# The rotary sum of queries and keys, moved from VectorE to an accumulating transfer on GpSimd's queue

## The chip, the cores and the metric

The kernel runs on one core of a Trainium2 chip. The metric is the time of one execution on the device in microseconds, the median of several runs. A profiled execution gives the span, which runs from the first to the last instruction, and the trace that is read below.

## What is computed

Attention over 8 batches, 8 heads, 576 positions and 64 dimensions, with a rotary embedding on queries and keys, followed by a soft mixture of 8 experts with 4 slots each:

```python
def rotate(x):
    x1, x2 = (x[..., :half], x[..., half:])
    return np.concatenate([x1 * cos - x2 * sin, x1 * sin + x2 * cos], axis=-1)
q_rot, k_rot = (rotate(q), rotate(k))
scores = scale * np.matmul(q_rot, k_rot.transpose(0, 1, 3, 2))
attn = softmax(scores); out = np.matmul(attn, v)     # cut
# then, with x = out as 4608 x 512:
logits = x @ phi                                     # 512 x 32
slot_input = softmax(logits, axis=0).T @ x
slot_out[e] = np.maximum(slot_input[e] @ w1[e], 0) @ w2[e]
result = softmax(logits, axis=1) @ slot_out
```

The rotary part is what the change touches: each of q and k is a sum of two products, the vector by cosines and its two halves swapped by signed sines.

## The kernel before

The 64 heads are taken as 32 pairs; the two heads of a pair lie in the two halves of the 128 partitions. The attention stage is a software pipeline written out by hand. A table WHEN gives every task of a pair a moment, counted in quarter pairs relative to the moment when the first block of exponentials of that pair is due; four quarter pairs are one beat, the time in which the pipeline moves on by one pair. In every beat the tasks are issued in the order of their moment modulo 4, each for the pair that is due there. Each engine runs its own instructions strictly in that order, and the transfers that one engine issues stand in that order between its other instructions.

For one pair the tasks around the change are these, in the order of their moments:

- load0 and load1 (-15.9, -14.496): SyncE (SP) issues one transfer each, 576 KB, for the queries and for the keys. A tile x_in holds both, and for each of them the vector and its swapped copy, side by side. There are two x_in tiles, so a load waits until the pair two before has been read by low.
- spin0 and spin1 (-13.466, -12.4): GpSimd multiplies x_in in place by the table of cosines and sines, in four pieces for the queries and four for the keys (L140).
- join (-9.9): VectorE adds the two products, for queries and keys at once (L144).
- high0 and high1 (-9.4817, -9.0595): ScalarE casts the sums to float16, hl (L149).
- low (-8.0): VectorE subtracts the cast from the sum, which gives the low half as float16 (L153). This is the last use of the pair's x_in.
- the tasks m.. and t0 to t8: TensorE computes scores from hl. For the m tasks VectorE takes their maxima (L175); for the t tasks ScalarE takes exponentials (L221). The tasks share three PSUM tiles.

```python
def spin(p, t, eng, cols):
    x = loaded[p][:, t]
    for c in cols:
        eng.tensor_tensor(out=x[:, :, c], in0=x[:, :, c], in1=cs_sb[:, :, c], op=ALU.mult)

def join(p, t=slice(0, 2), c=full):
    x = loaded[p]
    nc.vector.tensor_tensor(out=x[:, t, 0, c], in0=x[:, t, 0, c], in1=x[:, t, 1, c], op=ALU.add)

def high(p, t, c=full):
    ...
    nc.scalar.copy(out=halves[p][:, 1 + t, c], in_=loaded[p][:, t, 0, c])
```

Behind the attention of a pair, its softmax is normalized. ScalarE copies the sums of the exponentials out (L270), SP sends them into a tile rc (task send, L276), VectorE adds and inverts them (task recip, 7.294, L282 and L283), SP writes the reciprocals to DRAM (spread, 7.31, L289) and reads them back spread over the partitions into rb (widen, 7.3768, two transfers, L296), and GpSimd multiplies the pair's output by rb (norm, 8.706, L299).

Two moments matter for what follows. Modulo 4 norm stands at 0.706, and high0 at 2.518; load0 stands at 0.1, so SP issues it right behind widen, which stands at 3.377 of the beat before.

The start is outside the table. Pair 0 and pair 1 are loaded, multiplied, added and cast by lines of their own, with the additions on VectorE. The spins of pair 2 are issued there too. Then all tasks of the pairs 2 and 3 and so on whose moment lies before zero are issued in the order of the table, moment by moment:

```python
for when, name in sorted((when, name) for name, when in WHEN.items()):
    for p in range(NPAIR):
        if when + 4 * p < 0:
            do(name, p)
```

After the attention stage come the experts: weights from DRAM, two layers, and the output in pieces. This stage is not changed.

Of the kernel before, what the change touches and what calls it, by code (L numbers as in the profile page):

```python
# [11 lines left out]
ALU = mybir.AluOpType  # L12
# [32 lines left out]
RC = 12  # L45
PIECE = 4
WHEN = {
    "load0": -15.9, "load1": -14.496, "spin0": -13.466, "spin1": -12.4, "join": -9.9, "high0": -9.4817, "high1":
    -9.0595, "low": -8.0, "m01": -6.5262, "m10": -5.894, "m00": -5.0601, "m11": -4.7, "load_v": -3.85, "m20": -3.771,
    "m21": -3.317, "m30": -2.9, "m31": -2.7, "m_rem": -2.6642, "m_min": -2.49, "m_turn": -1.744, "m_half": -1.667,  # L50
# [13 lines left out]
def attn_softmoe(ctx, tc, qk, v, phi, w1, w2, cs, ident, sel, seg, out):  # L64
    nc = tc.nc
# [56 lines left out]
    loaded = {}  # L122
# [23 lines left out]
    def high(p, t, c=full):  # L146
        if p not in halves:
            halves[p] = stk.tile([P, 4, S], F16, name="hl")
        nc.scalar.copy(out=halves[p][:, 1 + t, c], in_=loaded[p][:, t, 0, c])  # L149
# [390 lines left out]
    def fast(task):  # L540
# [4 lines left out]
        "load1": lambda p: fetch(p, 1),  # L545
        "spin0": lambda p: spin(p, 0, nc.gpsimd, parts),
        "spin1": lambda p: spin(p, 1, nc.gpsimd, parts),
        "join": join,
        "high0": lambda p: high(p, 0),
        "high1": lambda p: high(p, 1),  # L550
        "low": low,
# [116 lines left out]
    p = NPAIR - 1  # L668
# [265 lines left out]
```

## Time and profile before

| | |
|---|---|
| time, median of 3 runs | 616.39 us (612.28 to 619.03) |
| the profiled execution | 613.56 us, of which 611.8 us are the span |
| mean granted TensorE clock | 0.959 |
| busy, share of the span | TensorE 87%, VectorE 81%, ScalarE 53%, GpSimd 52% |
| transferred | 111.63 MB, 182 GB/s over the span |

In the rows of the profile PE is TensorE, PEld its weight loads, DVE VectorE, ACT ScalarE, POOL GpSimd, SP SyncE; a name with a q behind it is that engine's sequencer, which issues transfers. A row of the timeline gives the start, the duration in us, the engine, the line of the kernel, the operation, what it writes and reads, how many instructions are merged, and in brackets how long the engine was idle before it and what ended that wait. In a row of windows stand the window, its length, the busy time of PE, PEld, DVE, ACT and POOL, the granted clock, the busy share of the DMA engines and GB/s.

### The profile page before, as it was taken

Reading aid. Unit: us, or ns where it says so; the run is one execution under the profiler, and the core shown is the slowest. Engines: PE = TensorE matmul, PEld = TensorE weight load, DVE = VectorE, ACT = ScalarE, POOL = GpSimd, SP = SyncE. Lnnn points to the kernel's source line nnn. Section 1 sums busy time; section 2 is a strip of 40 time slices with the busy share of each in tenths; the row PEclk is TensorE's granted clock in tenths of the full one; section 3 lists DMA queues with packets and bytes.
Section 4 is the critical chain, followed back from the end, with each engine's and each line's share of the span. In section 5 each row is a group of like instructions: output and inputs, shape, how many; then the busy total and the mean of one; then the engine's idle time right before and its main releaser. Section 6 shows DMA issues by size and latency. Waiting matters only on the chain.

```text
span 611.8 us, 23277 instructions
## 1 busy us (share of the span) xinstructions
PE 532.9 (87%) x10064; PEld 352.1 (58%) x10064; DVE 497.0 (81%) x729; ACT 326.9 (53%) x647; POOL 315.1 (52%) x308
## 2 busy tenths in 40 slices
PE   3668999998999899989999899898898999799981
PEld 2346666656765566666656565666566666443551
DVE  6879899999998999999998999999899874322341
ACT  2145656665665565656656566565465655324441
POOL 2668498655676566647763857658654000100000
PEclk9679999999999999999999999999899999859996
DMA  7153555555555555555555555455542246649999
GB/s 260 60 195 119 175 174 173 174 174 173 174 173 174 174 174 174 173 175 174 174 173 175 173 174 174 174 174 174 171 141 62 64 130 206 206 142 350 349 376 298
DMA packets 71734, 111.63 MB, mean 182 GB/s; under 512 B 20176, under 2 KB 47568, under 8 KB 71632
## 3 DMA queue, kind: packets, MB, share of 16 engines
q1 hardware_dynamic: 71618, 110.15, 54.5%
q8 instruction: 79, 1.29, 0.9%
q14 instruction: 23, 0.19, 0.1%
q10 hardware_dynamic: 14, 0.00, 0.0%
HBM read 99.93 MB, written 9.58 MB: 179 GB/s over the span
## 4 chain that ended last, share of the span: by engine, by line
PE 35%; DVE 26%; DMA 20%; ACT 6%; SPq 5%; issue 5%; POOL 1%; DVEq 0%; ACTq 0%
PE s_ps L220 8%; PE o_ps L236 8%; DVE nm L175 7%; DMA rc<-s 7%; DMA w_exp<-in_w 6%; DVE c_t L253 6%; DVE hl L153 5%; SPq L276 4%; ACT a_t L221 3%; PE s_ps L265 3%; DMA x_in<-in_qk 3%; PE s_ps L773 3%; DMA v_in<-in_v 2%; DVE c_t L255 2%; PE s_ps L173 2%
## 5 line engine op out<-in xcount | busy, mean ns | idle before, releaser
L140 POOL TENSOR_TENSOR x_in<-x_in,cs_sb 128x288 f32<-128x288 f32 x248 | 264.9, 1101 | 63.0 <-DMA x_in<-in_qk 38.1
L221 ACT ACTIVATE a_t<-s_ps 128x576 f32<-128x576 f32 x256 | 158.9, 649 | 97.8 <-PE s_ps L220 95.9
L175 DVE TENSOR_REDUCE nm<-s_ps 128x2 f32<-128x576 f32 x256 | 187.1, 743 | 15.1 <-PE s_ps L173 14.9
L236 PE MATMUL o_ps<-a_t,v_in 64*64 64x288 f32 x2048 | 172.4, 413 | 1.0 <-ACT xt L244 0.3
L220 PE MATMUL s_ps<-hl 64*64 64x288 f16 x3456 | 155.5, 286 | 16.4 <-DVE nm L175 15.9
L220 PEld LDWEIGHTS <-hl 64*64 64x64 f16 x3456 | 104.4, 107 | 59.9 <-issue 43.8
L299 POOL TENSOR_TENSOR xt<-xt,rb 128x576 f32<-128x576 f32 x30 | 42.8, 1425 | 141.0 <-DMA rb<-r_row 104.1
L173 PE MATMUL s_ps<-hl 64*64 64x288 f16 x1024 | 82.1, 298 | 26.0 <-DVE nm L175 20.5
L220 PE MATMUL s_ps<-peak,lift 64*64 64x288 f16 x1152 | 89.1, 284 | 0.0
L236 PEld LDWEIGHTS o_ps<-a_t,v_in 64*64 64x64 f32 x2048 | 72.9, 133 | 21.0 <-issue 7.3
L173 PEld LDWEIGHTS <-hl 64*64 64x64 f16 x1024 | 45.0, 107 | 49.1 <-issue 37.7
L149 ACT CAST hl<-x_in 128x576 f16<-128x576 f32 (+1 forms) x66 | 40.1, 650 | 33.1 <-DVE x_in L144 30.3
L270 ACT ACTIVATE s<-s_ps,bits 128x576 f32<-128x576 f32 x32 | 23.7, 740 | 58.0 <-PE s_ps L265 26.3
L144 DVE TENSOR_TENSOR x_in<-x_in 128x1152 f32<-128x1152 f32 (+2 forms) x36 | 53.4, 1483 | 0.5 <-POOL x_in L140 0.4
L253 DVE TENSOR_TENSOR c_t<-c_t,a_t 128x1152 f32<-128x1152 f32 x32 | 51.6, 1611 | 0.0
L153 DVE TENSOR_TENSOR hl<-x_in,hl 128x1152 f16<-128x1152 f32 x32 | 49.5, 1546 | 1.8 <-ACT hl L149 1.8
L253 DVE TENSOR_TENSOR c_t<-a_t 128x1152 f32<-128x1152 f32 x32 | 50.6, 1582 | 0.0
L220 PEld LDWEIGHTS <-lift 64*64 64x64 f16 x1152 | 38.1, 108 | 0.6
L265 PE MATMUL s_ps<-c_t,pick 128*32 128x288 f32 x256 | 37.1, 411 | 0.0
L265 PE MATMUL s_ps<-a_rem,pick 128*32 128x288 f32 x128 | 36.9, 411 | 0.0
L265 PE MATMUL s_ps<-a_t,pick 128*32 128x288 f32 x128 | 36.9, 411 | 0.0
L221 ACT ACTIVATE a_rem<-s_ps 128x576 f32<-128x576 f32 x32 | 20.8, 651 | 17.0 <-PE s_ps L220 17.0
(183 smaller groups left out, 597.6 us busy)
## 6 DMA issues: line engine op xcount, KB each, us to landing
x_in<-in_qk SPq DMA_DIRECT2D x62, 576.0 KB
w_exp<-in_w SPq DMA_DIRECT2D x63, 512.0 KB
v_in<-in_v SPq DMA_DIRECT2D x32, 576.0 KB
rb<-r_row SPq DMA_DIRECT2D x60, 144.0 KB
out<-w_exp SPq DMA_DIRECT2D x16, 512.0 KB
rc<-s SPq DMA_DIRECT2D x120, 4.5 KB
x_in<-in_qk SPq DMA_DIRECT2D x4, 288.0 KB
out<-w_exp SPq DMA_DIRECT2D x4, 256.0 KB
```

The lines of the kernel that those rows point to most:

```text
L140: eng.tensor_tensor(out=x[:, :, c], in0=x[:, :, c], in1=cs_sb[:, :, c], op=ALU.mult)
L144: nc.vector.tensor_tensor(out=x[:, t, 0, c], in0=x[:, t, 0, c], in1=x[:, t, 1, c], op=ALU.add)
L149: nc.scalar.copy(out=halves[p][:, 1 + t, c], in_=loaded[p][:, t, 0, c])
L153: nc.vector.tensor_tensor(out=hl[:, 0:4:3], in0=x[:, :, 0], in1=hl[:, 1:3], op=ALU.subtract)
L173: nc.tensor.matmul(s[rows[c], h, 0:HC], lhsT=hl[rows[h], QH, at:at + D], rhs=hl[rows[h], KH, half[n]], start=True, stop=True)
L175: nc.vector.tensor_reduce(out=nms[p][:, n, j:8:4], in_=s[:, :, 0:HC], axis=AX.X, op=ALU.max, negate=True)
L220: nc.tensor.matmul(s[rows[h ^ n], n, 0:HC], lhsT=lhs, rhs=rhs, start=(i == 0), stop=(i == 3))
L221: nc.scalar.activation(out=weights_of(p, b).rearrange("p (n x) -> p n x", n=2), in_=s[:, :, 0:HC], func=AF.Exp, scale=SCALE)
L236: nc.tensor.matmul(o[rows[h], n, 0:HC], lhsT=vt[r, b, n], rhs=a[r, half[n]], start=(b == 0), stop=(b == KB - 1))
L253: nc.vector.tensor_tensor(out=c, in0=c if j > 1 else ats[p, 0], in1=a, op=ALU.add)
L265: nc.tensor.matmul(s[32 * i:32 * i + 32, n, 0:HC], lhsT=pick[:, n:n + NS], rhs=m[:, half[n]], start=True, stop=True, tile_position=(0, 32 ...
L299: eng.tensor_tensor(out=xts[p], in0=xts[p], in1=rbs.pop(p), op=ALU.mult)
```

## The change

The sum of the two products is no longer an instruction on VectorE. It is a transfer that GpSimd issues: its source is the second product in x_in, its destination the first product in the same tile, and it adds to what stands there. The task's moment goes from -9.9 to -11.2, 1.3 quarter pairs forward. The first two pairs, whose lines stand outside the table, keep their addition on VectorE, so 30 of the 32 pairs are changed.

```diff
 WHEN = {
-    ... "join": -9.9, ...
+    ... "join": -11.2, ...
...
-        "join": join,
+        "join": lambda p: nc.gpsimd.dma_start(out=loaded[p][:, :, 0], in_=loaded[p][:, :, 1], accum_op=ALU.add),
```

The order of TensorE's and SP's instructions stays as it was, and so does that of ScalarE's; what its casts wait for is now the transfer. GpSimd's order changes at two kinds of place. At the start, behind the constants, it read before (L140 are the products, L299 is norm):

```order
L140 TENSOR_TENSOR x_in<-x_in,cs_sb 128x2x144 x40
L299 TENSOR_TENSOR xt<-xt,rb 128x576
L140 TENSOR_TENSOR x_in<-x_in,cs_sb 128x2x144 x8
L299 TENSOR_TENSOR xt<-xt,rb 128x576
L140 TENSOR_TENSOR x_in<-x_in,cs_sb 128x2x144 x8
```

and now reads, with the transfers as L548:

```order
L140 TENSOR_TENSOR x_in<-x_in,cs_sb 128x2x144 x24
L548 DMA x_in<-x_in 128x2x576 x2
L140 TENSOR_TENSOR x_in<-x_in,cs_sb 128x2x144 x8
L548 DMA x_in<-x_in 128x2x576
L140 TENSOR_TENSOR x_in<-x_in,cs_sb 128x2x144 x8
L299 TENSOR_TENSOR xt<-xt,rb 128x576
L548 DMA x_in<-x_in 128x2x576
```

The first 24 products are those of pairs 1, 2 and 3, eight each; the two transfers behind them are those of pairs 2 and 3, so pair 2's stands behind the products of pair 3. From the last two rows on, every beat has the same three rows in this order: the eight products of a pair, the norm of an earlier pair, and then the transfer of the pair whose products stand ahead of norm.

On VectorE the additions are gone. Its piece from the first subtractions (L153) to the first maxima of a new pair, before and now:

```order
L153 TENSOR_TENSOR hl<-x_in,hl 128x2x576
L144 TENSOR_TENSOR x_in<-x_in 128x2x576
L153 TENSOR_TENSOR hl<-x_in,hl 128x2x576
L175 TENSOR_REDUCE nm_276<-s_ps 128x2 x4
L183 TENSOR_REDUCE nm_276<-s_ps 128x2
```

```order
L153 TENSOR_TENSOR hl<-x_in,hl 128x2x576 x2
L175 TENSOR_REDUCE nm_276<-s_ps 128x2 x4
L183 TENSOR_REDUCE nm_276<-s_ps 128x2
L175 TENSOR_REDUCE nm_444<-s_ps 128x2
L187 TENSOR_REDUCE nm<-nm_276 128x9
```

The addition of pair 2 stood between the subtractions of pairs 1 and 2; now the two follow each other, and the second waits for pair 2's casts alone.

More of the change, by code (lines that the diff above doesn't have):

```diff
@@ L47 @@
 WHEN = {
-    "load0": -15.9, "load1": -14.496, "spin0": -13.466, "spin1": -12.4, "join": -9.9, "high0": -9.4817, "high1":
+    "load0": -15.9, "load1": -14.496, "spin0": -13.466, "spin1": -12.4, "join": -11.2, "high0": -9.4817, "high1":
     -9.0595, "low": -8.0, "m01": -6.5262, "m10": -5.894, "m00": -5.0601, "m11": -4.7, "load_v": -3.85, "m20": -3.771,
```

## Prediction

> **What bounds the kernel now.** I read the page first, then one row of windows over the even middle of the attention stage, then the groups by form.
>
> ```profile
> span 611.8 us, 23277 instructions
> PE 532.9 (87%) x10064; PEld 352.1 (58%) x10064; DVE 497.0 (81%) x729; ACT 326.9 (53%) x647; POOL 315.1 (52%) x308
> ...
> 100.00:400.00 300.00, 275.18 (x5725) 187.35 (x5723) 285.04 (x406) 181.98 (x362) 195.29 (x183) 1.00 0.51 170
> ...
> L144 DVE TENSOR_TENSOR x_in<-x_in 128x1152 f32<-128x1152 f32 x30 | 49.4, 1648 | 0.4 <-POOL x_in L140 0.4
> L299 POOL TENSOR_TENSOR xt<-xt,rb 128x576 f32<-128x576 f32 x30 | 42.8, 1425 | 141.0 <-DMA rb<-r_row 104.1 <-ACT a_t L221 17.6 <-DVE nm L175 13.0
> ```
>
> Over the whole span TensorE is the busier engine, but from 100 to 400 us it is VectorE: 285.04 of 300 us (95%) against 275.18 (92%) on TensorE, 61% on ScalarE and 65% on GpSimd. The DMA engines are busy half the time. The 30 rotary additions that the change takes from VectorE cost 49.4 us there, 1.65 us each. The last row is GpSimd's normalization (norm): before its 30 executions the engine sat idle for 141 us, mostly for the transfer that brings the reciprocals, rb. That wait matters below.
>
> How long is a beat (one head pair)? The first and the last norm of the even stretch stand 26 beats apart:
>
> ```profile
> 67.65 1.41 POOL L299 TENSOR_TENSOR xt<-xt,rb 128x576 f32<-128x576 f32 x1 [5.86 <-DMA rb<-r_row]
> ...
> 470.44 1.41 POOL L299 TENSOR_TENSOR xt<-xt,rb 128x576 f32<-128x576 f32 x1 [6.38 <-ACT a_t L221]
> ```
>
> (470.44 - 67.65) / 26 = 15.49 us. At 95% VectorE is busy 14.7 us of it, at 92% TensorE 14.2. Without the addition VectorE needs 14.7 - 1.65 = 13.1, so TensorE becomes the floor: I take 14.4 us, its 14.2 and a few waits that remain. That is the most the edit can give, 1.1 us a beat, 29 us over the 27 beats.
>
> **What is moved, and behind what.** One beat from the timeline of all engines but TensorE:
>
> ```profile
> 213.03 0.22 DVE L282 TENSOR_REDUCE rr<-rc 96x12 f32<-96x48 f32 x1
> 213.53 0.34 SPq L289 DMA_DIRECT2D r_row<-rr  x1
> 215.02 2.06 SPq L296 DMA_DIRECT2D rb<-r_row  x2
> 211.50 4.97 POOL L140 TENSOR_TENSOR x_in<-x_in,cs_sb 128x288 f32<-128x288 f32 x4 [0.61 <-DMA x_in<-in_qk]
> 217.18 0.53 SPq L135 DMA_DIRECT2D x_in<-in_qk  x1
> 218.75 0.42 SPq L135 DMA_DIRECT2D x_in<-in_qk  x1
> 219.75 1.41 POOL L299 TENSOR_TENSOR xt<-xt,rb 128x576 f32<-128x576 f32 x1 [3.28 <-DMA rb<-r_row]
> 221.64 4.18 POOL L140 TENSOR_TENSOR x_in<-x_in,cs_sb 128x288 f32<-128x288 f32 x4 [0.48 <-DMA x_in<-in_qk]
> 222.68 1.73 DVE L144 TENSOR_TENSOR x_in<-x_in 128x1152 f32<-128x1152 f32 x1
> 224.72 1.23 ACT L149 CAST hl<-x_in 128x576 f16<-128x576 f32 x2
> 227.10 4.18 POOL L140 TENSOR_TENSOR x_in<-x_in,cs_sb 128x288 f32<-128x288 f32 x4 [1.28 <-DMA x_in<-in_qk]
> 227.78 0.23 DVE L282 TENSOR_REDUCE rr<-rc 96x12 f32<-96x48 f32 x1
> 228.80 1.82 DVE L153 TENSOR_TENSOR hl<-x_in,hl 128x1152 f16<-128x1152 f32 x1
> ```
>
> The products of this pair end at 211.50 + 4.97 = 216.47, the addition on VectorE runs at 222.68 and ScalarE casts the sum at 224.72. There are 8 us to spare, if the transfer left right behind the products. It does not: in the order of GpSimd norm stands between them, and norm, waiting for rb, ends at 219.75 + 1.41 = 221.16. From there to the cast, which ScalarE reaches without a wait, only 3.56 us remain. Behind the issuing instruction on GpSimd stand the next products (221.64); what it takes to issue delays them, but the second half waits for its load until 227.10 anyway and ends at 231.28, before the next norm needs the engine, so I cost that at nothing. If that cover were gone, it would move norm itself.
>
> **How long the transfer takes** no row shows: nothing here is issued by GpSimd's queue or accumulates. The nearest rows:
>
> ```profile
> 225.60 2.05 DMA rc<-s
> ...
> DMA  3211000010101511995999989999984220010010
> GB/s 114 39 12 8 4 1 0 0 8 2 33 0 60 198 37 28 226 157 143 387 385 374 357 295 335 390 415 406 438 350 176 40 39 6 8 36 1 0 9 0
> ```
>
> A 4.5 KB transfer inside SBUF takes 2.05 us from issue to landing. The two lines are 210 to 230 us in slices of 0.5 us: the loads that SP issues from 217.18 on fill all engines from about 218 to 225 us, at some 375 GB/s. The low end is a copy of 576 KB alone: 2.05 + 590 / 375 = 3.6 us. The first load of the burst took 221.64 - 217.18 = 4.5 us, the last, behind three others, 227.10 - 218.75 = 8.35 us; both are 576 KB too. The sum has to read both operands, twice 1.57 us, and at 221.2 it enters in the middle of the burst, where I assume that it gets half the rate: 2.05 + 3.15 + 3.15 = 8.35. I take **8.35 us**, the row of the last load. The high end is that and two more passes over its own bytes, 11.5 us, if the add itself or the issue on GpSimd is slow. The collision is built in: the loads follow the rb transfers on SP's queue, and norm follows their landing.
>
> The Trainium skill (DMA: Bandwidth & Descriptors, "Anatomy of one DMA — SWDGE (gpsimd) path") fits such a transfer at 2.0 us plus its bytes at 436 GB/s, 3.35 us here as an estimate; by it the even beats would run at their floor, as in the first rival below. The Trainium skill (Collectives: The Full Stack, "The bandwidth ceiling: the fold count and why AG ≠ RS ≠ AR") says that an add in a DMA runs at half the rate of a copy since it reads two sources, which speaks for the other side; no run shows either yet.
>
> **The beat that follows.** Call T the beat and D the time from issue to landing. The reciprocals start 227.78 - 224.72 = 3.06 us after ScalarE reaches the cast, norm ends 221.16 - 213.03 = 8.13 us after them, so the next transfer leaves 11.2 us after the cast was reached and lands at 11.2 + D, while the next cast is reached after T. ScalarE then waits S = 11.2 + D - T with all exponentials behind it. Part of that is free: VectorE's queue holds 228.80 - 224.72 - 1.23 = 2.85 us of work ahead of the subtraction that needs no cast. So T = 14.4 + S - 2.85, and with S put in, T = 11.4 + D / 2, never under 14.4. With D = 8.35: T = **15.55**, S = 4.0. Gain and wait cancel: 27 x 0.06 = +1.6 us.
>
> **The start** is where the order costs something definite.
>
> ```profile
> 20.00:40.00 20.00, 12.49 (x151) 8.29 (x154) 14.32 (x19) 5.24 (x9) 10.63 (x14) 0.67 0.34 117
> ...
> 31.30 1.35 DVE L144 TENSOR_TENSOR x_in<-x_in 128x1152 f32<-128x1152 f32 x1
> 31.40 4.26 SPq L135 DMA_DIRECT2D x_in<-in_qk  x3
> 32.68 1.24 ACT L149 CAST hl<-x_in 128x576 f16<-128x576 f32 x2 [6.01 <-DVE x_in L144]
> 33.83 1.18 ACT L221 ACTIVATE a_t<-s_ps 128x576 f32<-128x576 f32 x2
> 35.33 17.18 POOL L140 TENSOR_TENSOR x_in<-x_in,cs_sb 128x288 f32<-128x288 f32 x16 [9.37 <-DVE hl L153]
> ...
> 39.82 1.56 POOL x_in L140 x2
> ...
> 41.41 1.94 DVE L144 TENSOR_TENSOR x_in<-x_in 128x1152 f32<-128x1152 f32 x1 [0.38 <-POOL x_in L140]
> 43.38 1.24 ACT L149 CAST hl<-x_in 128x576 f16<-128x576 f32 x2 [1.06 <-DVE x_in L144]
> ...
> DMA  0000459999946389997999632000000000001009
> ```
>
> Before, VectorE adds pair 2 at 31.30 and ScalarE casts it at 32.68, ahead of the first exponentials of the kernel (33.83). Pair 2's products had long been done (35.33 - 9.37 = 25.96), but its transfer now stands behind the eight products of pair 3, which need loads issued at 31.40 and end at 39.82 + 1.56 = 41.38. The last line, 30 to 50 us in slices of 0.5 us, shows idle DMA engines from 42.5 us on, so it lands some 4.8 us later (between 3.6 and 2.05 + 3.15 = 5.2, rounded up), at 46.2, and every exponential, and TensorE behind them, starts 13.5 us late. Pair 3's transfer follows directly and lands before its cast is reached, 43.38 - 33.83 = 9.6 us later. VectorE, rid of two additions, may regain half a microsecond: **+13 us**. Ends: 12, and 18 if TensorE, idle that long, falls back to the granted clock of 0.67 of this stretch.
>
> **Sum**, against the profiled execution of 613.56 us (span 611.8): 613.6 + 13 + 1.6 = 628.2. The median of the three runs lies 2.8 us above that execution, so I put the time at 631.
>
> **Rivals.**
> - *The transfer is short* (D of 6.0 or less): ScalarE's wait fits in the 2.85 us, T = 14.4, 27 x 1.1 = 29 us gained, 13 lost at the start: 600 on the same footing, faster. For it: the unloaded 3.6 us and the 4.5 of the first load. Against: it starts in the full burst. Between, each us of D is worth 13.5 us; D from 6.8 to 7.7 ends within 1% of before, which is about what a measurement of this kernel can tell from no change.
> - *The transfer is slow* (D about 11.5): T = 17.15, +45 and +13: 674. For it: two reads and a write per element, and an issue on GpSimd that no row prices. Against: 50% idle DMA time, though not at this place.
> - *The change doesn't do what it says*: the transfer does not leave behind its products but behind norm. That is what I forecast; were norm's wait to end early, with rb landing sooner once VectorE is lighter, the issue moves to 216.5 and D loses its weight: the first rival's time.
>
> **How the numbers follow.** Forecast, D from 7.7 to 10, 623 to 654: 0.42. Short transfer, or the issue moved forward: 0.20. Within 1%: 0.17. Slow: 0.21. Faster by over 1% is then 0.20, within 1% 0.17, slower 0.63. The range runs from 602, in the first rival, to 672, short of the slowest end.
>
> **What would show it.** Right: the first exponentials at about 47 instead of 33.8 us; ScalarE's cast group waiting for a transfer of x_in, 3 to 5 us in most beats; VectorE below 90% from 100 to 400 us; GpSimd's issues right behind norm; norms 15 to 16 us apart. Wrong: norms 14.4 apart with no wait at the cast (short), or DMA engines over 90% busy and norms 17 apart (slow). The start is wrong if the first exponentials stand where they stood.

## The result, and the profile after

| | before | after |
|---|---|---|
| time, median | 616.04 us (4 runs) | 704.3 us (4 runs, 694.02 to 716.36) |
| profiled execution / span | 613.56 / 611.8 us | 706.64 / 704.9 us |
| mean granted TensorE clock | 0.959 | 0.903 |

The change makes the kernel slower: the ratio is 1.133, with a 95% interval of 1.118 to 1.149. Executions of one kernel come out in a faster and a slower state, and the ratio and the times in the tables below are of the fast runs alone, which for the changed kernel are 694.02 and 701.96 us (median 698.0), while its profiled execution, from which the parts below are read, is a slow one. The direction is the predicted one, the size is not: 82 us (698.0 - 616.0) where 15 were forecast, and 698 lies outside the range of 602 to 672.

From the page of the changed kernel: the span, the engines, the DMA queues and the chain that ended last.

```profile
span 704.9 us, 23296 instructions
PE 563.6 (80%) x10064; PEld 367.1 (52%) x10064; DVE 464.3 (66%) x699; ACT 327.2 (46%) x647; POOL 297.0 (42%) x338
q0 software_dynamic: 8160, 17.70, 14.1%
PE 37%; DMA 32%; DVE 8%; ACT 8%; SPq 4%; issue 4%; POOL 3%; ACTq 0%; DVEq 0%; POOLq 0%
```

VectorE is down from 497.0 to 464.3 us, as intended. The new software queue q0 carries 17.70 MB, and the chain that ended last now runs for 32% of the span through transfers, where it was 20% before. The even middle in one row of windows, 100 to 400 us:

```profile
100.00:400.00 300.00, 251.93 (x4885) 167.88 (x4877) 227.49 (x324) 154.35 (x305) 152.84 (x168) 0.93 0.63 179
```

And from the waits of the whole run, those that grew (engine, line, what it waited for: total us, times, longest):

```profile
POOL xt L299 <- DMA rb<-r_row: 150.3, 21, 14.4
ACT hl L149 <- DMA x_in<-x_in: 110.5, 24, 21.0
...
POOL x_in L140 <- DMA x_in<-in_qk: 84.3, 31, 10.2
...
DVE rr L282 <- DMA rc<-s: 27.6, 21, 3.8
```

VectorE is now busy for 76% of this stretch (95% before) and TensorE for 84% (92%); TensorE's granted clock is 0.93 instead of 1.00, and the DMA share rose from 0.51 to 0.63. ScalarE waits at the cast for the new transfer, as forecast. But two other waits for transfers grew too, which the prediction left as they were: GpSimd's wait for the loads, from 38.1 to 84.3 us, and its wait for rb, from 104.1 to 150.3.

The span grew by 93.1 us. The first cast of pair 4 and of pair 31, 27 beats apart, cut it in three:

```profile
74.50 1.24 ACT L149 CAST hl<-x_in 128x576 f16<-128x576 f32 x2 [3.55 <-DMA x_in<-x_in]
...
565.13 1.23 ACT L149 CAST hl<-x_in 128x576 f16<-128x576 f32 x2
```

Before, the same two casts start at 57.66 and 473.89 us. So the start costs 74.50 - 57.66 = 16.8 us; the beat goes from 15.42 to (565.13 - 74.50) / 27 = **18.17 us**, 74.4 us in all; and what follows costs 1.9 us. The beats of the experiments are taken between the same two casts.

### The profile page after: what moved, and what is told of

Same layout as the page of the kernel before. It is cut to its first block, busy times and chain, and to the rows that moved or that the text cites. A ratio compares the mean times of both kernels' runs of the same rounds, so it can differ in the third digit from the quotient of the medians.

```text
span 704.9 us, 23296 instructions
## 1 busy us (share of the span) xinstructions
PE 563.6 (80%) x10064; PEld 367.1 (52%) x10064; DVE 464.3 (66%) x699; ACT 327.2 (46%) x647; POOL 297.0 (42%) x338
## 3 DMA queue, kind: packets, MB, share of 16 engines
q0 software_dynamic: 8160, 17.70, 14.1%
## 4 chain that ended last, share of the span: by engine, by line
PE 37%; DMA 32%; DVE 8%; ACT 8%; SPq 4%; issue 4%; POOL 3%; ACTq 0%; DVEq 0%; POOLq 0%
DMA x_in<-x_in 15%; PE s_ps L220 11%; PE o_ps L236 9%; DMA rb<-r_row 4%; DMA rc<-s 4%; ACT a_t L221 3%; SPq L276 3%; DMA w_exp<-in_w 3%; PE s_ps L265 2%; PE s_ps L773 2%; DMA r_row<-rr 2%; PE s_ps L334 2%; POOL xt L299 2%; PE s_ps L173 2%; DVE nm L175 2%
## 5 line engine op out<-in xcount | busy, mean ns | idle before, releaser
L140 POOL TENSOR_TENSOR x_in<-x_in,cs_sb 128x288 f32<-128x288 f32 x248 | 218.8, 1015 | 95.6 <-DMA x_in<-in_qk 84.3
L220 PE MATMUL s_ps<-hl 64*64 64x288 f16 x3456 | 169.7, 305 | 58.1 <-ACT a_t L221 47.8
L236 PE MATMUL o_ps<-a_t,v_in 64*64 64x288 f32 x2048 | 181.9, 434 | 4.8 <-ACT a_t L221 2.8
L220 PEld LDWEIGHTS <-hl 64*64 64x64 f16 x3456 | 112.7, 115 | 105.8 <-issue 87.8
L299 POOL TENSOR_TENSOR xt<-xt,rb 128x576 f32<-128x576 f32 x30 | 43.6, 1452 | 213.1 <-DMA rb<-r_row 150.3
L173 PE MATMUL s_ps<-hl 64*64 64x288 f16 x1024 | 82.2, 300 | 42.3 <-ACT a_t L221 21.5
L149 ACT CAST hl<-x_in 128x576 f16<-128x576 f32 (+1 forms) x66 | 40.3, 654 | 131.0 <-DMA x_in<-x_in 110.5
L220 PE MATMUL s_ps<-peak,lift 64*64 64x288 f16 x1152 | 93.8, 301 | 0.5 <-issue 0.5
L236 PEld LDWEIGHTS o_ps<-a_t,v_in 64*64 64x64 f32 x2048 | 74.5, 139 | 33.5 <-issue 11.9
L173 PEld LDWEIGHTS <-hl 64*64 64x64 f16 x1024 | 42.5, 108 | 66.0 <-issue 54.6
L153 DVE TENSOR_TENSOR hl<-x_in,hl 128x1152 f16<-128x1152 f32 x32 | 44.0, 1374 | 20.8 <-ACT hl L149 20.8
L253 DVE TENSOR_TENSOR c_t<-a_t 128x1152 f32<-128x1152 f32 x32 | 47.2, 1476 | 0.0
L253 DVE TENSOR_TENSOR c_t<-c_t,a_t 128x1152 f32<-128x1152 f32 x32 | 45.0, 1406 | 0.0
L548 POOL DMA_DIRECT2D x_in<-x_in x30 | 36.4, 1214 | 4.7 <-issue 4.4
L255 DVE TENSOR_TENSOR c_t<-c_t,a_t 128x576 f32<-128x576 f32 x32 | 31.8, 995 | 1.4 <-ACT a_t L221 1.3
```

Source lines behind the costliest of these rows:

```text
L153: nc.vector.tensor_tensor(out=hl[:, 0:4:3], in0=x[:, :, 0], in1=hl[:, 1:3], op=ALU.subtract)
L173: nc.tensor.matmul(s[rows[c], h, 0:HC], lhsT=hl[rows[h], QH, at:at + D], rhs=hl[rows[h], KH, half[n]], start=True, stop=True)
L220: nc.tensor.matmul(s[rows[h ^ n], n, 0:HC], lhsT=lhs, rhs=rhs, start=(i == 0), stop=(i == 3))
L236: nc.tensor.matmul(o[rows[h], n, 0:HC], lhsT=vt[r, b, n], rhs=a[r, half[n]], start=(b == 0), stop=(b == KB - 1))
L253: nc.vector.tensor_tensor(out=c, in0=c if j > 1 else ats[p, 0], in1=a, op=ALU.add)
L299: eng.tensor_tensor(out=xts[p], in0=xts[p], in1=rbs.pop(p), op=ALU.mult)
```

## The experiments

Two theories were set against each other: **A**, the loss is the wait at the cast, because the transfer stands behind norm, with what follows from that wait; **B**, the loss is the transfer's own traffic, wherever it stands. Each ratio goes by runs of the kernel before that were made beside it; their medians lie between 611.5 and 615.8 us.

**Place, start and floor.** Four kernels: the transfer ahead of norm in GpSimd's order; the sums of pairs 2 and 3 back on VectorE, which mends the start; both; and the kernel before without any sum, which bounds what relief of VectorE can give.

```diff
# ahead of norm, in the changed kernel
-    "join": -11.2
+    "join": -11.4
# start, in the changed kernel
+    "join_v": -9.9
+    "join_v": lambda p: p in (2, 3) and join(p)
+    "join": lambda p: p >= 4 and <the transfer>
# no sum, in the kernel before
-    "join": join
+    "join": lambda p: None
```

> The transfer's moment is -11.4 instead of -11.2, so that it stands ahead of norm in GpSimd's order, right behind its products; all else as in the changed kernel, the start too. Theory A (the beat is long because the transfer leaves behind norm, ScalarE waits some 3.7 us for it in every beat, and the TensorE clock halves after such waits): the wait at the casts goes, the beat falls from 17.6 us to 14.4 to 15.3, the half-clock stretches between 76 and 557 us (68 us in all) nearly vanish, and the time falls from 704 to 625 to 645 us; the 15 us of the start stay. Theory B (the transfer's own traffic, two reads and a write of 576 KB in each beat, slows the loads and the small transfers wherever it stands): the beat stays at 17 us or more and the time above 685 us.

> The changed kernel with pairs 2 and 3 added on VectorE at their old moment (-9.9); all later pairs by the transfer behind norm. The start's step of the prediction: the first exponentials stand at about 34 us again instead of 49, and the time falls by 13 to 16 us, to 688 to 691. If the start is absorbed later, by the beats or the expert stage, the time stays within 4 us of 704.

> Both: the transfer ahead of norm (-11.4) and pairs 2 and 3 on VectorE. Theory A: the two effects add, 610 to 630 us, which may lie below the 616 us of the kernel before if the beat comes under 15.4 us. Theory B: above 670 us.

> The kernel before with the sum of pairs 2 to 31 left out (neither VectorE nor a transfer adds, so queries and keys are wrong). It gives the beat that is to be had when VectorE is rid of the addition and nothing takes its place. The prediction's floor is 14.4 us, 29 us below the kernel before: 585 to 590 us. If TensorE or the order of tasks holds the beat at 15 us or more anyway, 600 us or more, and then no placing of the transfer can win much.

| | time, median | ratio to before (95%) | beat |
|---|---|---|---|
| ahead of norm | 675.3 us | 1.098 (1.088 to 1.108) | 16.98 |
| start | 690.9 us | 1.126 (1.118 to 1.134) | 17.97 |
| both | 663.4 us | 1.079 (1.072 to 1.086) | 17.01 |
| no sum | 602.0 us | 0.979 (0.974 to 0.984) | 15.05 |

The start costs about what was predicted. Mending it brings the cast of pair 4 forward by 11.7 us (from 74.50 to 62.83), and by 11.9 with the earlier place (from 73.72 to 61.87); the times fall by 7.1 and by 11.9 us, where 13 to 16 were expected. The floor was too low: without the sum the beat is 15.05 us, not 14.4, so all that VectorE's relief can bring in this order of tasks is 2.1%. The earlier place takes off 1.2 us a beat, not the 3 that A wanted, and leaves 2 us above the floor. But it is no clean trial of A, since it shortens the wait at the cast and does not end it. ScalarE's wait for the transfer, in the kernel ahead of norm:

```profile
ACT hl L149 <- DMA x_in<-x_in: 63.4, 12, 20.8
```

Without the 20.8 us of the start these are 42.6 us in 11 beats, against 89.5 in 23 in the changed kernel. What the wait and the traffic cost had to be taken apart.

**Taking the two apart.** One kernel has the transfer without the wait, the next a hold at the cast without the transfer. The third replaces the accumulation by a plain copy. The fourth, with the transfer ahead of norm and the start mended, gives it a third x_in tile and so one beat more until its cast.

```diff
# transfer that nobody waits for, in the changed kernel
-    dma_start(out=loaded[p][:, :, 0], in_=loaded[p][:, :, 1], accum_op=ALU.add)
+    dma_start(out=loaded[p][:, :, 1], in_=loaded[p][:, :, 0], accum_op=ALU.add)
# long cast, in the kernel before, behind the first cast of a pair, from pair 2 on
+    for _ in range(5): nc.scalar.copy(out=halves[p][:, 1, c], in_=loaded[p][:, 0, 0, c])
# plain copy, in the changed kernel
-    accum_op=ALU.add
# third tile, ahead of norm and with the start mended
-    "load0": -15.9, "load1": -14.496, "spin0": -13.466, "spin1": -12.4, "join": -11.2
+    "load0": -19.9, "load1": -18.496, "spin0": -17.466, "spin1": -16.4, "join": -15.4
-    name="x_in", bufs=2        # and N_W = 25
+    name="x_in", bufs=3        # and N_W = 22
```

> The changed kernel's accumulating transfer, at its place and of its size, but it adds the first half of each tile into the second, which nothing reads: no cast waits for it (only the next load into that tile, which comes after the subtraction anyway). The sum itself is done nowhere for pairs 2 to 31, as in the run that leaves it out (602.0 us, beat 15.05). Theory A (the loss comes from ScalarE's wait at the cast and from the half clock behind that wait; the transfer as such costs little): 600 to 608 us, beat 15.0 to 15.3, no half clock. Theory B (its traffic on the DMA engines and its issue on GpSimd lengthen the beat whoever waits): 620 us or more, beat 15.7 or more, reciprocals and loads late as in the changed kernel.

> The kernel before, with ScalarE repeating the first cast of each pair from 2 on five times (3.1 us of ScalarE, the same values written again): a hold of the changed kernel's mean length at the same place, without any transfer. Theory A (a hold of 3 us at the cast costs most of its length and then TensorE's half clock): 640 to 670 us, beat 16.3 to 17.4, 30 us or more of half clock. Theory B, and the prediction's sum (2.85 us of such a hold are free, so the loss in the changed kernel is traffic): 616 to 626 us, beat 15.4 to 15.8, next to no half clock.

> The changed kernel with a plain copy in place of the accumulating one: same place, same issue, same waits, half the reads (the result lacks the product that the copy overwrites). If the second read is what makes the transfer long: landing 5.5 to 7 us after issue instead of 8.6, beat 16.5 to 17.2, 660 to 685 us. If issue on GpSimd and the queue's fixed part make up the 8.6 us: landing above 8, beat 18 or more, 695 to 705 us.

> Transfer ahead of the normalization, pairs 2 and 3 added by VectorE, and a third input buffer per pair, so that loads, products and the transfer of a pair all run one beat earlier (three of the 25 prefetched weight tiles give up their memory for it): the transfer has one more beat until its cast, its traffic per beat is unchanged. Theory A (wait and clock): no wait at the cast, no half clock, beat 15.0 to 15.4, 602 to 615 us. Theory B (traffic): beat 16.5 or more as with the transfer ahead of the normalization and two buffers, 645 us or more.

| | time, median | ratio to before (95%) | beat |
|---|---|---|---|
| unawaited | 670.2 us | 1.095 (1.089 to 1.100) | 17.13 |
| long cast | 664.7 us | 1.088 (1.079 to 1.097) | 17.06 |
| plain copy | 656.3 us | 1.072 (1.065 to 1.079) | 16.60 |
| third tile | 661.7 us | 1.083 (1.076 to 1.089) | 16.70 |

Both mechanisms are there. A transfer that no cast waits for still costs 2.08 us a beat over the floor (27 x 2.08 = 56 us; 14 of its 68 us are the start, where a load waits for the transfer). With the third tile no cast waits either, and the beat is still 16.70: that is B. (Its start and end, with other loads first and fewer weights, cost more, so only the beat is compared.) A hold at the cast with no transfer at all costs 17.06 - 15.42 = 1.64 us a beat: that is A. The hold lasted 3.5 us, not the 3.1 expected, as the row of the five repeated casts shows:

```profile
63.07 3.49 ACT L152 CAST hl<-x_in 128x576 f16<-128x576 f32 x5
```

The plain copy lands after 7.6 us, outside the 5.5 to 7 expected, and its 656.3 us are under the 660 to 685, but its beat of 16.60 is in the range and shows that the accumulation, with its second read, is dear.

How does a transfer that nobody waits for lengthen the beat? First SP's issues of the small transfers rc in the kernel without the sum, and VectorE's step that needs them:

```profile
264.37 2.73 SPq L276 DMA_DIRECT2D rc<-s  x4
...
268.66 0.23 DVE L282 TENSOR_REDUCE rr<-rc 96x12 f32<-96x48 f32 x1 [0.19 <-DMA rc<-s]
```

And the same with the unawaited transfer, with VectorE's next row maxima and TensorE's next scores:

```profile
257.18 6.60 SPq L276 DMA_DIRECT2D rc<-s  x4
...
265.34 0.23 DVE L282 TENSOR_REDUCE rr<-rc 96x12 f32<-96x48 f32 x1 [3.80 <-DMA rc<-s]
...
265.75 0.69 DVE L175 TENSOR_REDUCE nm<-s_ps 128x2 f32<-128x576 f32 x1
...
266.49 0.32 PE L220 MATMUL s_ps<-hl 64*64 64x288 f16 x4 [3.43 <-DVE nm L175]
```

The four issues take 6.60 us instead of 2.73, VectorE stands at L282 for 3.80 us until their data is there, the row maxima behind it are late, and TensorE waits 3.43 us for them. From the last issue to VectorE's step it is 1.56 us in both, so it is the issues that are late, and not the small transfers behind them. The DMA engines in the same two stretches, 250 to 290 us without the sum in slices of 1 us, and 250 to 285 with the unawaited transfer in slices of 0.875 us:

```profile
DMA  0000000147889999520000038699999520001996
```

```profile
DMA  0408898999999994100004989999999999310000
```

In the first the burst of loads runs from 258 to 267 us, and the issues of rc at 264.37 meet its end. In the second it runs from 252.6 to about 263, and the issues at 257.18 fall into it. Over the whole run VectorE's wait for rc, from the waits without the sum and with the unawaited transfer:

```profile
DVE rr L282 <- DMA rc<-s: 9.8, 19, 1.7
```

```profile
DVE rr L282 <- DMA rc<-s: 52.3, 26, 3.8
```

**Two remedies.** One moves VectorE's step on the reciprocals behind the subtraction, so that its wait holds less, in the unawaited kernel, in a control without the sum, and in the version with both the earlier place and the mended start. The other leaves the three tiles and issues the transfer three quarters of a beat later, between the two groups of products of the next pair.

```diff
# reciprocals later
-    "recip": 7.294, "spread": 7.31, "widen": 7.3768
+    "recip": 8.05, "spread": 8.06, "widen": 8.07
# three tiles, later place
-    "join": -15.4
+    "join": -12.5
```

> The run with the transfer that nobody waits for (670.2 us, beat 17.13), with VectorE's step on the reciprocals moved behind the subtraction and one addition of the denominators, and SP's two issues that follow from it moved along; GpSimd's order is the same. Theory B1 (the traffic makes the four small transfers of the denominators land 2 to 4 us later, VectorE's queue stands at the reciprocals until then, and the subtraction and row maxima behind it hold TensorE): beat 15.2 to 15.8, little half clock, 620 to 636 us (14 us of start stay, since there a load waits for the transfer). Theory B2 (the traffic acts through the large loads and GpSimd's own time, not through VectorE's queue): beat 16.6 or more, 655 us or more.

> Control: the kernel before with the sums of pairs 2 to 31 left out (602.0 us, beat 15.05) and the reciprocals moved behind the subtraction as in the run beside this one. Both theories: 600 to 610 us, beat 15.0 to 15.4. Under 597 us, the move would be a gain of its own, and over 615 us a loss of its own, and the run beside it would have to be read against this one.

> Transfer ahead of the normalization, pairs 2 and 3 added by VectorE (663.4 us, beat 17.01), and the reciprocals moved behind the subtraction. Theory B1: the beat loses the hold at the reciprocals, and the waits at the cast that follow from late loads remain: 15.7 to 16.3, 628 to 646 us. Theory B2: 655 us or more, beat 16.7 or more.

> Three input buffers as before (661.7 us, beat 16.70, transfer issued just ahead of the normalization), with the transfer issued later by three quarters of a beat, between the two groups of products of the next pair, about where the DMA engines are idle and past the load burst, some 3 us ahead of the next small transfers. If the place matters (less overlap with loads and small transfers): beat 16.0 or less, 645 us or less. If it is the sum of the traffic in the beat, wherever it stands: 16.5 to 16.9, 655 to 667 us.

The times are 694.1 (ratio 1.131, 1.122 to 1.141), 629.9 (1.028, 1.021 to 1.036), 715.0 (1.165, 1.154 to 1.177) and 666.0 us (1.084, 1.073 to 1.095). The first remedy fails, and the control says why the time of the run beside it can't be read by itself: the move alone costs 28 us without any transfer (629.9 - 602.0). With the unawaited transfer it costs 24 us (694.1 - 670.2), and with both the earlier place and the mended start 52 (715.0 - 663.4). The load burst that SP issues behind the reciprocals comes later and runs into the next rc by itself: the four issues last 5.4 us on average in the control, 2.9 before the move. But VectorE does not wait for rc at all in the control; TensorE now waits 10.7 us for norm (at L348) and 12.7 for the transfers of the row maxima, peak, and did not before. Which of these makes the 28 us is not shown.

Read against its control, the unawaited kernel with the move still says something. VectorE's wait for rc there:

```profile
DVE rr L282 <- DMA rc<-s: 11.4, 8, 2.7
```

It is 11.4 us instead of 52.3, and yet the transfer costs 17.94 - 16.11 = 1.83 us a beat over the control, little less than the 2.08 before the move. So the hold at L282 that was seen above is one path by which the traffic acts, and the loss does not hang on it alone.

The later place gives 666.0 us where the earlier one gave 661.7. That was not the idle place that was meant, as these rows of SP, GpSimd and VectorE show:

```profile
251.12 2.72 SPq L277 DMA_DIRECT2D rc<-s  x4
...
252.32 1.18 POOL L550 DMA_DIRECT2D x_in<-x_in  x1
...
258.45 0.23 DVE L283 TENSOR_REDUCE rr<-rc 96x12 f32<-96x48 f32 x1 [3.24 <-DMA rc<-s]
```

The transfer was to leave 3 us ahead of rc, and it leaves a median of 1.3 us behind the first issue of rc. The issues are as quick as without any sum (2.72 us here), but from the last of them to VectorE's step it is now 258.45 - 253.84 = 4.6 us instead of 1.56. So this place gains nothing, and the transfer meets rc there directly; whether another place would gain is not shown.

**Bytes, or GpSimd?** Two kernels take the prefetched weights, 512 KB a beat, out of the burst, one is the control for that, and one adds a store of about the bytes that the transfer reads, issued by SP in each beat.

```diff
# light: unawaited, changed kernel, and no sum
-    "weights": lambda p: p >= 2 and len(w_tiles) < N_W and load_w(wp, N_W)
+    "weights": lambda p: p == 28 and [load_w(wp, N_W) for _ in range(N_W)]
# plain store, in the kernel without the sum, behind the load of v, for pairs 3 to 30
+    sink = dram.tile([P, 2, 2, S], F32, name="sink")
+    nc.sync.dma_start(out=sink, in_=cs_sb.unsqueeze(1).broadcast_to([P, 2, 2, S]))
```

> The transfer that nobody waits for (beat 17.13 us, 670.2 us), with the 512 KB of weights that each beat prefetches taken out of the beats: all 25 are loaded behind pair 28 instead, so the end is longer and only the beats up to pair 26 are compared. If the transfer's bytes are the cause, because they keep the load burst running into the next small transfers: giving back 1.4 us of DMA time per beat brings the beat to 15.2 to 16.0 and the four issues of the small transfers from 5.0 back to 3.0 to 3.5 us. If GpSimd's issue or its hold on VectorE is the cause, whatever the DMA engines carry: 16.8 or more.

> The kernel before without the sums of pairs 2 to 31 (beat 15.05 us, 602.0 us), with one store of 1,152 KB per beat from SBUF to a scratch area that nothing reads, issued by SP between the loads: about the bytes that the accumulating transfer reads, but no GpSimd, no accumulation and no wait. If bytes are the cause: beat 16.4 to 17.6, 635 to 670 us. If the kind of transfer or GpSimd is the cause: 15.0 to 15.4, 600 to 612 us.

> The changed kernel with the weights of the attention stage loaded behind pair 28 (the same comparison, beats up to pair 26 only; its beat was 18.17 us). If bytes in the load burst are the cause, for the loads and so for the products and the wait at the cast: 16.4 to 17.2, transfer landing 7 us or less. If not: 17.8 or more.

> Control: the kernel before without the sums of pairs 2 to 31 and with the weights behind pair 28; beats up to pair 26. The beat is 15.05 us with the weights; if 512 KB less changes nothing there, 14.9 to 15.1: the burst ends in time as it is. If 14.7 or less, the DMA engines bound that kernel too.

Beats from pair 4 to pair 26, the 22 that the late weights leave alone:

| | with the weights | without |
|---|---|---|
| no sum | 15.09 | 14.77 |
| unawaited | 17.06 | 16.25 |
| changed kernel | 18.23 | 17.70 |
| no sum, plain store | 17.63 | |

The store shows that bytes are enough: 665.8 us (ratio 1.084, 1.068 to 1.100) and a beat of 17.63, with no GpSimd and no accumulation in it. Windows of the even middle, of the kernel without the sum, of the one with the store and of the unawaited transfer:

```profile
100.00:400.00 300.00, 281.23 (x5875) 190.78 (x5871) 260.55 (x394) 184.43 (x368) 178.47 (x185) 1.00 0.52 175
```

```profile
100.00:400.00 300.00, 253.82 (x5061) 170.90 (x5050) 225.72 (x337) 159.11 (x313) 159.51 (x159) 0.97 0.65 219
```

```profile
100.00:400.00 300.00, 257.20 (x5164) 173.22 (x5156) 230.91 (x343) 163.74 (x322) 161.89 (x182) 0.97 0.66 190
```

The DMA share, 0.65 and 0.66 against 0.52, and TensorE's busy time, 254 and 257 us against 281, are nearly the same for the store and the transfer. VectorE's wait for rc is too (61.2 and 52.3 us over the whole run). The other waits are not: under the store GpSimd waits 178.5 us for loads, under the transfer 57.2, and without the sum 74.8. The store stands on SP's own queue between the loads, so the two need not slow the beat along the same path.

The other way round, 512 KB less give back 0.8 us a beat under the unawaited transfer, where 1.1 to 1.9 were expected, and 0.5 in the changed kernel, where 1.0 to 1.8 were. (The kernel with the mended start, whose beats have the same instructions as the changed kernel's, has 17.94 in this table's beats; against it only 0.2 come back.) The beat of 16.25 lies between what was expected of bytes, 16.0 or less, and of GpSimd, 16.8 or more. The four issues of rc go from 5.1 to 3.7 us on average, where 3.0 to 3.5 were expected, and the changed kernel's transfer still lands after 8.6 us, where 7 or less was expected. The control gains 0.3 as well, so part of what these bytes cost has nothing to do with the new transfer; over the control the transfer costs 1.48 us a beat without the weights and 1.97 with them. The three light kernels end later, at 687.3, 721.8 and 626.2 us, since the weights then load at the end. No version here that computes the sum by a transfer is faster than the kernel before.

## Why the prediction was wrong in size

**The start: right.** Forecast were 13 us and the first exponentials at about 47 us:

```profile
47.81 1.24 ACT L149 CAST hl<-x_in 128x576 f16<-128x576 f32 x2 [21.02 <-DMA x_in<-x_in]
48.96 1.18 ACT L221 ACTIVATE a_t<-s_ps 128x576 f32<-128x576 f32 x2
```

They stand at 48.96 instead of 33.83, 15.1 us later, and pair 4's cast is 16.8 us late.

**The length of the transfer: right in its total, not in its parts.** The group of issues with the median from issue to landing (the last number), in the changed kernel and with the plain copy:

```profile
x_in<-x_in POOLq DMA_DIRECT2D x30, 576.0 KB, 8.6
```

```profile
x_in<-x_in POOLq DMA_DIRECT2D x30, 576.0 KB, 7.6
```

8.6 us against the 8.35 of the sum. But the sum had 3.15 us for each of two reads, so a copy, with one, should have landed after 2.05 + 3.15 = 5.2 us, and it took 7.6. That the total came out is luck in part. In engine time the two reads do show. The queue q0 with the plain copy:

```profile
q0 software_dynamic: 4320, 17.70, 6.9%
```

It takes 6.9% of 656.3 us for 30 copies, 1.5 us each on all 16 engines; the accumulating transfers take 14.1% of 704.9 us, 3.3 us each, about twice as much. By the rule of the Trainium skill (Collectives: The Full Stack, "The bandwidth ceiling: the fold count and why AG ≠ RS ≠ AR") on adds with two sources this was to be expected, and the trace agrees. The estimate of 3.35 us by the Trainium skill (DMA: Bandwidth & Descriptors, "Anatomy of one DMA — SWDGE (gpsimd) path") is far from the 8.6 measured here. So the rival of a short transfer falls.

**The beat: three terms of T = 14.4 + S - 2.85 failed.** In the order of their size:

1. *The transfer slows nobody else.* The sum followed one transfer along one path, from norm to the cast, and took the times of loads, rc and rb from the profile of before. It had the 3.15 us of engine time in its own line, as part of D, and not in anyone else's. But the load burst, rc, reciprocals and rb follow one another round the beat, and 3.3 us more of engine time come on top; the late issues of rc are the one path of this that the traces show. Price, from the unawaited run: 27 x (17.13 - 15.05) = 56 us.
2. *Of the wait, 2.85 us are free.* S itself was near, though by luck: ScalarE waits (110.5 - 21.0) / 23 = 3.9 us in each of the later beats in which it waits, and 4.0 was forecast. With the beat and the landing as measured, the formula would leave 11.2 + 8.6 - 18.2 = 1.6 us. The path ahead of the transfer had grown as well: the reciprocals start 4.3 us after the cast is reached, on average, and not 3.06, and norm ends 8.1 us after them, as forecast. The price of such a wait was wrong: the hold of 3.5 us alone, which by the formula should have cost 3.5 - 2.85 = 0.65 us, cost 1.64. The windows of the changed kernel show one reason, around a cast that started at 282.23 after 4.73 us of wait:

```profile
279.00:282.00 3.00, 1.21 (x24) 0.60 (x17) 1.24 (x2) 0.00 (x0) 0.18 (x1) 1.00 0.69 139
280.80:284.20 3.40, 0.13 (x5) 0.12 (x8) 1.40 (x4) 1.79 (x3) 2.38 (x4) 1.00 0.14 17
284.20:287.50 3.30, 3.30 (x33) 1.96 (x32) 2.99 (x2) 1.39 (x3) 1.78 (x1) 0.51 0.39 80
```

 TensorE runs dry in the wait (1.21 us busy of 3.00, then 0.13 of 3.40) and then, with work again, gets half its clock for 3.4 us. Such stretches sum to 72 us between the two casts above, against 3 before, to 34 under the long cast, and to 31 under the unawaited transfer, so the clock is a part of the price of both mechanisms. At half clock no more than half of the time is lost, so of these 72 us at most 36. The Trainium skill (TensorE: Matmul & The Clock Gate, "Part 1: The HAM clock gate (the "warmup" mystery)") gives an idle window of about 3.4 us for the fall to half; the stretches here last 3.4 or 6.8 us, which agrees in length, but in the 3.4 us before the 16 stretches of the changed kernel TensorE was busy for 0 to 1.6 us, and before only two of them was it not busy at all. The prediction had the clock only as an end of the start's range. Price of wait and clock on top of the traffic: 27 x (18.17 - 17.13) = 28 us, or 23 by the 17.97 of the kernel with the mended start.
3. *The floor of 14.4.* Busy time of TensorE per beat plus a guess was not a floor; without the sum the beat is 15.05. The relief is worth 27 x (15.42 - 15.05) = 10 us, not 29.

With the start and the end, 16.8 - 10 + 56 + 28 + 2 = 93 us, the whole difference of the two profiled spans (the medians differ by 82). It comes out by construction, since each part is the difference of two neighbouring measurements. It takes wait and traffic as if they add, which the runs do not show on their own. The split is one order of taking them away: ahead of norm, for instance, 1.2 us a beat went with the place alone.

**The rivals.** "Slow" came nearest with a beat of 17.15 us, for the wrong reason: D is not 11.5 us. The sign given for it, DMA engines over 90% busy, was wrong too: they are busy 63% on average, and in the beat shown above full just where the small transfers need them. The third rival, a transfer that leaves ahead of norm, was built as the first experiment and gave 675 us, not the 600 of the first rival: all of the traffic and part of the wait stay.

**Open.** That SP's four issues of rc last longer while the burst runs was seen; what holds them was not tested. By which path the traffic costs its 2 us a beat where VectorE hardly waits for rc is not known. Nor was it shown why 512 KB fewer bytes give back only 0.2 to 0.8 us. How much of the loss is clock alone was read from the trace and not measured by itself.

## What to carry to other kernels

Price a new transfer as a load on the DMA engines as well as a latency on its own path: ask which transfers lie before and after it in the beat, and who waits for the smallest of them. An average DMA share of 50% promised room that this beat did not have; moving the reciprocals and the transfers behind them by a fifth of a beat, with no byte added, already cost 28 us here. And before trading work off the busiest engine, leave that work out in one run: here it could give 2%.

## What the runs showed that was not expected

Two accumulating transfers that GpSimd issued one behind the other did not overlap. At the start the second was issued only after the first had landed, at 47.74 us:

```profile
42.27 1.36 POOL L548 DMA_DIRECT2D x_in<-x_in  x1
48.01 1.22 POOL L548 DMA_DIRECT2D x_in<-x_in  x1 [4.38 <-issue]
```

Two plain copies at the same place went out at once, one behind the other, and the second landed 1.65 us after the first (48.06 and 46.41 us):

```profile
42.84 1.67 POOL L548 DMA_DIRECT2D x_in<-x_in  x2
```

What holds the second accumulating transfer back is not shown.

And VectorE can be held while GpSimd works on products: a five-column step, 0.2 to 0.7 us in the kernel before, lasted until the products ended.

```profile
253.94 6.38 DVE L422 TENSOR_SCALAR cm<-cm 128x5 f32<-128x5 f32 x1
...
253.81 6.47 POOL L140 TENSOR_TENSOR x_in<-x_in,cs_sb 128x288 f32<-128x288 f32 x8
```

Seven steps of VectorE in the changed kernel are longer than their median before by more than 1.5 us, 23 us in all; the kernel before has none. The Trainium skill (SBUF — State Buffer, "Who interferes with whom") says that these two engines share a port pair under a lock, which agrees, but no run here tested it. The unawaited kernel has six such steps, 19 us in all, and the one ahead of norm and the one with the store have none, at beats of 16.98 and 17.63 us. So this hold may be a part of the loss in some kernels, and it is not what makes the loss.
